# A fused layernorm, dilated attention and channel MLP: nine more constant matmuls, another order of loads, and a new hand-written order table

## The chip, the cores and the metric

The kernel runs on one core of a Trainium2 chip. That core has five engines which run side by side: PE (TensorE, matrix products into PSUM), DVE (VectorE), ACT (ScalarE), POOL (GpSimd) and SP (SyncE), which here issues the transfers between the chip's main memory and its on-chip memory. Each engine takes its instructions strictly in the order in which the program lists them, and waits on semaphores for what other engines or transfers must deliver. The metric is the device time of one execution in microseconds (us); the median of several runs is given.

## The reference

`S` is 2048 tokens of `D` = 512 channels, `H` = 32 heads of 16, a window of 8 keys two positions apart, and an MLP of width `F` = 1376.

```python
x  = A_x
xn = _layernorm(x)                      # per token, over 512 channels
qkv = xn @ wqkv                         # 512 x 1536, split in q, k, v of 32 heads
idx = pos[:, None] - arange(8) * 2      # own position and seven earlier ones, two apart
logits = einsum("bhsd,bhswd->bhsw", q, k[idx]) * scale    # masked where idx < 0
o  = einsum("bhsw,bhswd->bhsd", softmax(logits), v[idx])
s  = o @ wo
y  = _layernorm(xn)
h  = _gelu(y @ w1 + b1)                 # 512 x 1376
g  = _silu(h @ w2 + b2)                 # 1376 x 512
return x + s * g
```

## The kernel before

**Tiling.** Because the keys lie two positions apart, even and odd tokens never meet. The tokens are split in two classes `c`, each of 8 tiles of 128 tokens. The heads are split in four blocks `hb` of 8 heads (128 channels). One pair (`c`, `hb`) is a unit; there are eight, 0 to 7. A unit's projection is made by `qkv` (line 883): per tile twelve matmuls (line 909) that give q, k and v together in a PSUM bank, then an eviction to the buffer `U` by ACT (line 927) or DVE (line 923). Its attention is made by `attention` (line 960) on DVE, with POOL for some sums and ACT for the exponential. The MLP runs in four chunks of 512 tokens and 11 slices of `F`: `mlp1` (lines 1188, 1201, 1204, 1206) gives one slice of gelu(h), `mlp2` (line 1231) adds its product with `w2`. `wo_first` and `wo_last` apply `wo`, multiply by the gate and add x.

**Precision.** Each operand of a large product is kept as two float16 halves, high and low, and three products are summed. High halves are made by ACT, DVE or POOL (`split`, lines 571, 573; line 635 for `wqkv`), low ones by DVE or POOL (lines 577, 642). Before a weight is split, the sum of its squares sets a power of two as its scale: ACT squares it (line 605 for `wqkv`), PE adds the squares over the partitions (line 521) and DVE makes the scale of it.

**The head.** Two tiles of class 0, tiles 6 and 7, are loaded already transposed (`t`, line 1303). Their mean over the channels is found by DVE and one PE product for tile 6 (lines 707, 716) and by four PE products for tile 7 (line 704); DVE subtracts it (line 719), and `direct` multiplies them in float32 with block 0 of `wqkv` as loaded (line 727, four steps each). The other six tiles (`x`, line 1278) are normalised (statistics on DVE, line 675; factors on POOL, line 760; scaling on lines 786, 790 or 793). Tiles 0 to 3 are transposed by PE (line 811) and split by ACT and DVE (lines 815, 818); tiles 4 to 7 are transposed by a transfer (line 803).

**Constant matmuls.** Line 1350 multiplies two constant tiles into the bank `z0`, 256 columns, `WAKE` times. No one reads the result. Line 1465 lets ACT compute one element with exp, gelu or silu, `NTAB` times each; where the function isn't the one last used, ACT loads another table ahead of it.

**Order.** Every operation is first added to a list, `Plan.ops`, and gets its place in it as its number. `Plan.issue` (line 291) then emits the operations in the order of the table `ORDER` (line 80), which is complete: 1290 numbers. It alone decides in which order each engine and SP's queue see their work, and which buffer of a ring an operation gets. Constants such as `EV0`, `EV1` and `W1ENG` say which engine does an operation; the tuple `LOADS` only sets the numbers of the loads.

Loads have the numbers 0 to 18, the zero fills of line 1285 are 108 and 109, the constant matmuls 110 to 128. So the head of the old table, `110, 6, 4, 37, 111, 38, ...`, is a constant matmul, the load of tile 7, the load of x tile 0, the statistics of tile 0, and so on. SP issues in it: tile 7, x0, tile 6, first half of block 0 of `wqkv`, x2, x1, second half of block 0, x5, b1, block 1, x4, x3, block 1's second half, then W1's last part, x7, x6 and the rest of W1.

Of the kernel before, what the change touches and what calls it, by code (L numbers as in the profile page):

```python
# [56 lines left out]
W1ENG = ('dve', 'act', 'act', 'act', 'act', 'act', 'act')  # L57
# [4 lines left out]
EV0 = ('act', 'act', 'dve', 'act', 'dve', 'dve', 'dve', 'dve')  # L62
EV1 = ('dve', 'dve', 'act', 'dve', 'act', 'act', 'act', 'act')
# [12 lines left out]
NTAB = (8, 12, 6)  # L76
# [299 lines left out]
PU1 = 0.969  # L376
PWARM = 0.9
PEV = 0.2698

PTOT = 0.5899  # L380

WAKE = 19
PS1 = 1.1561

QHI = 4

PQLO = 0.5225

# [1187 lines left out]
```

## Time and profile before

| what | value |
|---|---|
| median of 3 runs | 409.51 us (409.25 to 409.98) |
| profiled execution | 409.47 us |
| its span, first to last instruction | 407.7 us |
| time around the span | 1.8 us |
| granted TensorE clock, mean | 0.999 |

The profile is of one execution. Its views used below are the page with the busy time of each engine, the chain of work that ended last, the timeline (start, duration, engine, line, operation, output and inputs, count; in brackets the idle time before and what ended it), busy times by stretches, and groups of instructions by line. An instruction's duration in the timeline is from its start to its end; matmuls overlap, so their pace is read from start to start. `U` in a transfer from `in_A_xt` is a transposed tile, `prod` from `in_A_x` an x tile, `prod` from `in_A_wqkv` block 0.

### The profile page before, as it was taken

How to read it: one execution, taken by the hardware profiler on the slowest of the kernel's cores; microseconds unless marked ns; L12 is line 12 of the kernel's file. 1: busy time of each engine (PE TensorE's matmuls, PEld its weight loads, DVE VectorE, ACT ScalarE, POOL GpSimd, SP SyncE). 2: the span in 40 equal slices, each digit the busy share in tenths (PEclk: the TensorE clock that was granted, in tenths of full speed). 3: DMA queues.
4: the chain of work that ended last, by engine and by line, in shares of the span. 5: the costliest groups of instructions: out<-in, count | busy, mean ns of one | idle time of the engine just before them, and what ended most of it. 6: DMA issues, size and time to landing. Idle time of an engine off the chain costs nothing.

```text
span 407.7 us, 5541 instructions
## 1 busy us (share of the span) xinstructions
PE 400.9 (98%) x2030; PEld 198.3 (49%) x2030; DVE 378.7 (93%) x386; ACT 246.2 (60%) x413; POOL 134.1 (33%) x141
## 2 busy tenths in 40 slices
PE   7999999999999999999999999999999999999996
PEld 5665544444444455445544554444455444444443
DVE  5987999999999999999799999999799899999976
ACT  3999998895599866753595344224422195367160
POOL 4823001062752443044404425052507206250012
PEclk9999999999999999999999999999999999999999
DMA  7977481440026271944092008233312466008655
GB/s 270 411 164 224 157 226 40 126 149 17 2 49 154 48 157 52 195 78 57 2 185 86 0 2 213 82 130 103 92 37 79 91 168 162 0 1 141 202 153 208
DMA packets 52627, 48.04 MB, mean 118 GB/s; under 512 B 37066, under 2 KB 37510, under 8 KB 52088
## 3 DMA queue, kind: packets, MB, share of 16 engines
q1 hardware_dynamic: 52600, 47.69, 43.2%
q8 instruction: 16, 0.26, 0.3%
q14 instruction: 11, 0.09, 0.1%
HBM read 24.40 MB, written 7.34 MB: 78 GB/s over the span
## 4 chain that ended last, share of the span: by engine, by line
PE 97%; DMA 1%; DVE 1%; SPq 0%; issue 0%; DVEq 0%
PE ps L909 30%; PE ps L1188 26%; PE z L1231 25%; PE ps L1101 5%; PE z L1133 2%; PE ps L1133 2%; PE z L1219 2%; PE pl L909 1%; DMA U<-in_A_xt_dram 1%; PE z L727 1%; PE pl L1133 1%; PE pl L727 1%; PE z L1222 1%; PE z L811 1%; DVE U L1165 0%; DVE U L1172 0%
## 5 line engine op out<-in xcount | busy, mean ns | idle before, releaser
L909 PE MATMUL ps<-wq,yT 128*128 128x384 f16 (+1 forms) x708 | 129.6, 337 | 0.0
L1231 PE MATMUL z<-w,h 128*128 128x512 f16 x480 | 113.5, 379 | 0.0
L1188 PE MATMUL ps<-yT,w 128*128 128x512 f16 x480 | 109.2, 379 | 0.0
L909 PEld LDWEIGHTS <-yT 128*128 128x128 f16 x744 | 72.6, 98 | 58.6 <-issue 0.2
L975 DVE TENSOR_TENSOR prod<-U 128x2048 f32<-128x2048 f32 x32 | 73.1, 2285 | 1.4 <-DMA U<-U 0.5
L1188 PEld LDWEIGHTS <-w 128*128 128x128 f16 x480 | 46.6, 98 | 55.9 <-issue 0.9
L978 DVE TENSOR_REDUCE L<-prod 128x128 f32<-128x2048 f32 x32 | 73.0, 2282 | 0.6
L1231 PEld LDWEIGHTS <-h 128*128 128x128 f16 x480 | 46.6, 98 | 53.9 <-issue 0.2
L927 ACT ACTIVATE U<-ps,cs 128x384 f32<-128x384 f32 x56 | 31.3, 573 | 56.8 <-PE ps L909 56.8
L1044 POOL TENSOR_TENSOR prod<-prod,prod 128x1024 f32<-128x1024 f32 x14 | 38.5, 2770 | 79.7 <-DVE prod L1033 64.0
L1033 DVE TENSOR_TENSOR prod<-pl,U 128x2048 f32<-128x2048 f32 x28 | 63.5, 2283 | 0.3
L1201 ACT ACTIVATE ps<-ps,b1T,hsc 128x512 f32<-128x512 f32 x40 | 29.7, 747 | 27.8 <-PE ps L1188 27.5
L1204 ACT ACTIVATE h<-ps,hsc 128x512 f16<-128x512 f32 x40 | 27.1, 682 | 16.7 <-PE z L1231 15.0
L1054 POOL COPY gate<-prod 1x1 f32<-1x1 f32 x21 | 4.9, 231 | 97.4 <-DVE prod L975 90.4
L1055 POOL TENSOR_TENSOR prod<-prod 128x1024 f32<-128x1024 f32 x14 | 32.9, 2348 | 0.0
L1206 DVE SCALAR_TENSOR_TENSOR h<-ps,hsc,h 128x512 f16<-128x512 f32 x40 | 29.7, 743 | 2.1 <-ACT h L1204 2.0
L1101 PE MATMUL ps<-wo,oT 128*128 128x512 f16 x96 | 21.9, 379 | 0.0
L1028 DVE TENSOR_TENSOR prod<-prod,prod 128x2048 f32<-128x2048 f32 x9 | 20.6, 2283 | 0.1
L1201 ACT ACT_TABLE_LOAD x13 | 16.7, 1283 | 3.8 <-PE ps L1188 3.7
L1465 ACT ACT_TABLE_LOAD x14 | 18.0, 1283 | 0.2
L1016 ACT ACTIVATE o<-prod,osc 128x1024 f16<-128x1024 f32 (+1 forms) x9 | 9.5, 1050 | 14.0 <-DVE prod L1028 8.3
L1055 POOL TENSOR_TENSOR prod<-prod,prod 128x1024 f32<-128x1024 f32 x7 | 16.4, 2350 | 0.0
(201 smaller groups left out, 404.2 us busy)
## 6 DMA issues: line engine op xcount, KB each, us to landing
f<-in_A_x_dram SPq DMA_DIRECT2D x31, 256.0 KB, 4.9
U<-U SPq DMA_DIRECT2D x16, 392.0 KB, 4.3
gd<-f SPq DMA_DIRECT2D x12, 256.0 KB, 3.7
prod<-in_A_x_dram SPq DMA_DIRECT2D x8, 256.0 KB, 5.3
oT<-in_B_w_dram SPq DMA_DIRECT2D x2, 1024.0 KB, 7.4
yT<-in_B_w_dram SPq DMA_DIRECT2D x2, 1024.0 KB, 6.9
f<-gd SPq DMA_DIRECT2D x8, 256.0 KB, 2.7
out_dram<-f SPq DMA_DIRECT2D x8, 256.0 KB, 3.1
```

What stands on the lines that cost most here:

```text
L909: nc.tensor.matmul(b.t[:, 0:wide], y[:, s, k, o:o + P], wq[hb][:, t, k], start=(n == 0), stop=(n == 11))
L927: act(384, lambda i=i, b=b: nc.scalar.activation(U3[:, i:i + 31:15, :], b.t[:, 0:384].rearrange("p (t e) -> p t e", t=3), AF.Identity, sca ...
L975: dve(2048, lambda p2=p2, g=g: nc.vector.tensor_tensor(p2(), q, slots(Ut, KH, 2 * g), op=ALU.mult), qk + [("kh", ub, 0), ("kh", ub, 1), (" ...
L978: dve(2048, lambda pr=pr, g=g: nc.vector.tensor_reduce(L3()[:, 2 * g:2 * g + 2], pr.t.rearrange("p (r f d) -> p r f d", r=2, d=DH), AX.X, ...
L1033: dve(2048, lambda: nc.vector.tensor_tensor(pr.t.rearrange("p (r f d) -> p r f d", r=2, d=DH), A3()[:, 2 * g:2 * g + 2].rearrange("p r (f ...
L1044: pool(2.4, lambda n=n: nc.gpsimd.tensor_tensor(acc.t[:, n:n + 1024], acc.t[:, n:n + 1024], p1.t[:, n:n + 1024], op=ALU.add), [acc, p1], [ ...
L1055: nc.gpsimd.tensor_tensor(x.t[:, 0:1024], x.t[:, 0:1024], y(), op=ALU.add)
L1101: nc.tensor.matmul(b.t, oT[:, hb, i // 4, s, i % 4], wo[:, t, hb], start=(hb == 0 and n == 0), stop=(hb == last and n == 2))
L1188: nc.tensor.matmul(b.t[0:M], w1[:, s, f * 512 + k * M:f * 512 + (k + 1) * M], yT[ch][:, t, k], start=(n == 0), stop=(n == 11))
L1201: act(512, lambda: nc.scalar.activation(b.t[0:M], b.t[0:M], AF.Gelu_apprx_tanh, bias=b1T[0:M, f:f + 1], scale=hsc[0:M, 1:2]), [b, ("b1T",) ...
L1206: dve(512, lambda: nc.vector.scalar_tensor_tensor(lo()[0:M], b.t[0:M], hsc[0:M, 2:3], hi()[0:M], op0=ALU.mult, op1=ALU.subtract), [b, hk], ...
L1231: nc.tensor.matmul(z.t, hl[s][:, t * P:(t + 1) * P], w2[:, w, f], start=(f == 0 and n == 0), stop=False)
```

## The change

Only constants change. `WAKE` goes from 19 to 28. `NTAB` goes from (8, 12, 6) to (8, 13, 7). `EV0` and `EV1` give the evictions of units 0 and 1 to other engines: for unit 0 tile 1 goes from ACT to DVE, tiles 5 and 7 from DVE to ACT; for unit 1 tiles 0 and 1 go from DVE to ACT. `W1ENG` gives the first high part of W1 (512 columns) from DVE to ACT, the second (512) and the last (384) from ACT to DVE. `ORDER` is a new table of 1301 numbers; since nine constant matmuls are added, an operation numbered 129 or more before has a number higher by nine, and after the added activations by ten or eleven.

```diff
-W1ENG = ('dve', 'act', 'act', 'act', 'act', 'act', 'act')
+W1ENG = ('act', 'dve', 'act', 'act', 'act', 'act', 'dve')
...
-EV0 = ('act', 'act', 'dve', 'act', 'dve', 'dve', 'dve', 'dve')
-EV1 = ('dve', 'dve', 'act', 'dve', 'act', 'act', 'act', 'act')
+EV0 = ('act', 'dve', 'dve', 'act', 'dve', 'act', 'dve', 'act')
+EV1 = ('act', 'act', 'act', 'dve', 'act', 'act', 'act', 'act')
...
-NTAB = (8, 12, 6)
+NTAB = (8, 13, 7)
...
 ORDER = (
-    110, 6, 4, 37, 111, 38, 112, 40, 49, 113, 0, 1, 114, 3, 8, 32, 19, 115, 109, 116, 2, 117, 118, 119, 120,
-    121, 122, 123, 124, 125, 26, 27, 20, 128, 28, 7, 18, 5, 50, 21, 54, 53, 55, 51, 33, 52, 56, 10, 68, 22, 29,
...
+    110, 0, 108, 4, 1, 111, 112, 113, 114, 115, 2, 116, 117, 19, 244, 118, 109, 119, 120, 121, 37, 122, 123, 3,
+    124, 125, 32, 137, 130, 6, 131, 20, 134, 133, 132, 8, 21, 38, 40, 33, 5, 129, 22, 54, 34, 23, 35, 24, 36,
+    53, 26, 27, 47, 10, 41, 43, 49, 55, 25, 126, 50, 28, 56, 67, 136, 172, 51, 57, 42, 9, 29, 30, 7, 45, 11, 31,
...
-WAKE = 19
+WAKE = 28
```

Read with the numbers of the operations, the new table says this of the head. SP issues tile 6, x0, both halves of block 0, x2, tile 7, x1, block 1's first half, x4, x3, x5, block 1's second half, x6, a part of W1, x7, b1 and the rest of W1. PE does nineteen constant matmuls, the mean of tile 6 (20), four constant ones, the first direct step of tile 6 (22), the sum of the first squares of block 0 (34), a direct step (23), the second sum (35), a direct step (24), tile 7's mean (26), the last direct step of tile 6 (25), a constant matmul, tile 0's transposes (50), the four direct steps of tile 7 (28 to 31) with one constant matmul among them, the first four matmuls of tile 0, two constant ones, the sum of block 1's first squares, tile 1's transposes, a constant matmul, block 1's second sum, and tile 3's transposes. Tile 2's transposes come later. ACT squares both halves of block 0 first, scales three of its quarters, squares block 1's first half, casts tile 0, scales the fourth quarter, normalises tile 1 and squares block 1's second half.

At the end, `wo_last` takes the first part of tile 4's product before the matmuls that need the last half of `oT`; in the queue of SP the last V halo of unit 6 stands behind a transposing store to `oT`.

122 rows, old and new, of the table ORDER are left out of this document.

## The prediction

> **What bounds the kernel now.** I read the busy table first, then the chain of work that ended last.
>
> ```profile
> span 407.7 us, 5541 instructions
> PE 400.9 (98%) x2030; PEld 198.3 (49%) x2030; DVE 378.7 (93%) x386; ACT 246.2 (60%) x413; POOL 134.1 (33%) x141
> ...
> PE 97%; DMA 1%; DVE 1%; SPq 0%; issue 0%; DVEq 0%
> ```
>
> PE is both the busiest engine and the chain. A busy PE can hide gaps, since matmul ends are modelled, so the next views are the busy time by stretches, PE's long wait, and two pieces of the chain in order of time.
>
> ```profile
> 0.00:5.00 5.00, 3.81 (x23) 3.03 (x24) 1.34 (x5) 1.28 (x1) 1.03 (x9) 1.00 0.54 166
> 5.00:10.00 5.00, 3.35 (x17) 2.00 (x16) 4.15 (x10) 1.97 (x4) 3.42 (x3) 1.00 1.03 369
> 10.00:15.00 5.00, 5.00 (x26) 3.02 (x25) 4.69 (x21) 4.47 (x11) 3.67 (x5) 1.00 1.05 405
> 15.00:20.00 5.00, 4.97 (x33) 3.04 (x32) 4.79 (x15) 4.97 (x10) 4.92 (x5) 1.00 1.01 416
> 20.00:30.00 10.00, 10.00 (x64) 5.99 (x63) 8.30 (x20) 9.97 (x20) 2.95 (x3) 1.00 0.69 170
> 30.00:45.00 15.00, 15.00 (x89) 8.42 (x88) 12.86 (x25) 14.97 (x32) 3.57 (x2) 1.00 0.81 259
> 45.00:403.00 358.00, 357.98 (x1784) 172.36 (x1784) 340.72 (x294) 208.54 (x341) 114.57 (x116) 1.00 0.39 98
> ```
> ```profile
> PE ps L716 <- DVE f L707: 1.6, 1, 1.6
> ```
> ```profile
> 17.00 9.10 PE ps L909 x56
> ...
> 66.50 2.59 PE ps L1188 x12
> ```
>
> Columns after the stretch: its length, PE, PEld, DVE, ACT, POOL, clock, DMA share, GB/s. From 10 us on PE is full, and in the chain twelve 512-column matmuls take 2.59 us, 0.216 each, and a 384-column one 0.162 (9.10 by 56): full pace. Nothing after 20 us can be gained from PE, only lost. What the change can win lies in the first 17 us, and the tail. The timeline of that head:
>
> ```profile
> 1.19 3.26 PE L1350 MATMUL z<-first,fours 128*128 128x256 bf16 x16 [1.19 <-DVE first L448]
> ...
> 4.08 0.69 DVE L675 BATCH_NORM_STATS2 bn<-prod 128x6 f32<-128x512 f32 x1 [2.58 <-DMA prod<-in_A_x_dram]
> ...
> 4.28 1.06 PE L704 MATMUL ps<-U,first 128*128 128x128 f32 x8
> ...
> 5.90 1.02 DVE L707 TENSOR_REDUCE f<-U 128x128 f32<-128x512 f32 x1 [0.72 <-DMA U<-in_A_xt_dram]
> ...
> 6.85 1.35 DVE L719 TENSOR_TENSOR U<-U,ps 128x512 f32<-128x512 f32 x2
> ...
> 6.98 0.84 ACT L605 ACTIVATE wq<-prod 128x768 bf16<-128x768 f32 x1 [4.97 <-DMA prod<-in_A_wqkv_dram]
> ...
> 6.98 0.49 PE L716 MATMUL ps<-f,first 128*128 128x128 f32 x2 [1.65 <-DVE f L707]
> ...
> 7.58 0.91 PE L727 MATMUL z<-prod,U 128*128 128x384 f32 x2
> ...
> 9.41 0.81 PE L727 MATMUL z<-prod,U 128*128 128x384 f32 x2
> ...
> 10.05 0.27 PE L1350 MATMUL z<-first,fours 128*128 128x256 bf16 x1
> ...
> 12.49 0.66 PE L811 MATMUL z<-first,prod 128*128 128x128 f32 x4
> ...
> 12.98 0.81 PE L727 MATMUL z<-prod,U 128*128 128x384 f32 x2
> ...
> 16.37 0.63 PE L811 MATMUL z<-first,prod 128*128 128x128 f32 x4
> ...
> 16.83 3.41 PE L909 MATMUL ps<-wq,yT 128*128 128x384 f16 x20
> ```
>
> By start to start, two L727 take 0.64 us (9.41 to 10.05), four L811 or L704, the same shape, 0.44 to 0.49, one L909 0.162. So the useful work that PE has behind it at 16.83 is 8 L704 0.9, 2 L716 0.2, 16 L727 5.2, 16 L811 1.75, 8 L909 1.3, sums of squares 0.1: 9.4 us. **7.4 us are lost**: 1.19 before the first matmul, 3.09 of constant matmuls, 1.8 waiting for tile 6, the rest single constant matmuls and short waits. The change is worth what it does to these 7.4 us, plus what it loses later.
>
> **Loads.** Tile 6 comes first instead of third, tile 7 sixth instead of first, the head block third and fourth instead of fourth and seventh. The queue's bytes set the landing: in the old order the first block half lands at 6.98 (ACT started then) behind 1152 KB; in the new one 896 KB are ahead of its end, at 369 GB/s 0.7 us sooner, 6.27. In the same way, 256 KB per 0.71 us and 384 KB per 1.07: second half 7.3, x2 8.0, tile 7 8.75, x1 9.45; from 10 us at 405 GB/s: block 1 first half 10.4, x4 11.1, x3 11.7, x5 12.4, its second half 13.35. These are estimates from the rows above. Bytes in all are the same, and the MLP weights still end the burst.
>
> **Start of the direct matmuls.** Tile 6 now goes first and lands ahead of x0, which was there at 4.08; with its 1.02 the reduce L707 ends at 4.5 to 5.1. The nineteen constant matmuls now ahead of the mean L716 end at 4.6 (16 by 4.28, three more at 0.11, half a 512-column one). DVE does x0's statistics (0.69 and a short piece), then the subtract, half of L719's 1.35: about 6.1. The first L727 waits for the block: 6.3 instead of 7.58. But in the old order PE had already done tile 7's eight mean matmuls, in a hole; now they lie among the direct ones. Lost so far: 6.3 less 0.2 useful, 6.1.
>
> **Behind it.** The new order has PE's sums of squares of block 0 between the direct matmuls, so that PE waits for ACT:
>
> ```profile
> 7.73 0.19 ACT L605 ACTIVATION_READ_ACCUMULATOR wq<-prod 128x1 f32 x1
> ...
> 11.95 0.61 ACT L635 ACTIVATE wq<-prod,qsc 128x384 f16<-128x384 f32 x1
> ...
> 14.36 0.86 POOL L760 TENSOR_TENSOR rb<-pb,halves 128x3 f32<-128x3 f32 x1
> ...
> 15.49 0.54 DVE L793 TENSOR_SCALAR prod<-prod,mv,rb 128x512 f32<-128x512 f32 x1
> ```
>
> A square with its read takes 0.94 to 1.03 us. The first ends at 7.3, PE is there at 6.95 to 7.15 (0.2 lost); the second, landed at 7.3, ends at 8.35, PE is there at 8.0 (0.4 lost). Then PE runs on: two more direct steps, tile 7's mean at 9.1 (landed 8.75), tile 0's transposes, the four direct steps of tile 7, until 13.9. Five constant matmuls stand among them and behind at 0.11: 0.55. The four L635, 0.55 each, and the first q4 squares put the scaled block ready at 13.05, in time. Last, tile 3's transposes need x5: landed 12.4, statistics 0.9, factor L760 0.86, then two other DVE pieces and L793, 15.3 to 15.65, where PE arrives at 15.35: 0 to 0.3 lost. **Sum**: 6.1 + 0.2 + 0.4 + 0.55 + (0 to 0.3) = 7.25 to 7.55, and if the first direct step runs at a slower start after the idle stretch 0.2 more. Against 7.4 before, that is -0.15 to +0.35; I take +0.1. What the earlier start wins is given back to tile 7's mean, the squares and the constant matmuls.
>
> **The nine constant matmuls.** Three more than before stand ahead of the mean, hidden by the load and the reduce, and four in the hole behind it; in the dense part there are five where there were three, the 0.55 counted. The clock column is 1.00 in 5 to 10 us although PE had just sat idle 1.65. The Trainium skill (TensorE: Matmul & The Clock Gate, Part 1) says that the clock halves after an idle window of about 3.4 us. By that rule even a hole from 4.6 to 6.3 keeps the clock without any matmul, so the additions could only cost, and rival (d) below would have no chance; the one hole of this trace agrees, but stays below that window, so that I leave (d) a small one.
>
> **Engines moved.** Of the evictions three more go to ACT net, one W1 half comes in and two leave for DVE.
>
> ```profile
> L923 DVE TENSOR_SCALAR U<-ps,cs x3: 606/609/617, 29.4 to 35.7; 128x384 f32<-128x384 f32 x3
> ...
> L573 ACT ACTIVATE w<-oT,hsc x4: 704/1132/1132, 32.9 to 37.1; 128x1024 f16<-128x1024 f32 x3, 128x512 f16<-128x512 f32 x1
> ...
> L927 ACT ACTIVATE U<-ps,cs 128x384 f32<-128x384 f32 x56 | 31.3, 573 | 56.8 <-PE ps L909 56.8
> ```
>
> ACT: three at 0.57, less one W1 half of about 0.5 (the 512 one cancels): +1.2 us, in a stage, 15 to 45, in which it is idle 0.09 us of 30. DVE loses about as much. In the order table the PE pieces behind these are also moved later (tile 4's of unit 0 by 2 us of matmuls, tiles 4 and 5 of unit 1 by 5 to 8, though tiles 6 and 7 come 3 sooner), so most of the cover is there: I take 0.2, between 0 and 1.2.
>
> **Table loads.** Counting the changes of exp, gelu and silu down the old ACT order gives 38, as many as the trace has besides the first (14 and 13 in these rows, 11 in smaller groups); the new order gives 45, the two added activations included.
>
> ```profile
> L1465 ACT ACT_TABLE_LOAD x14 | 18.0, 1283 | 0.2
> L1201 ACT ACT_TABLE_LOAD x13 | 16.7, 1283 | 3.8 <-PE ps L1188 3.7
> ```
>
> Seven times 1.283 are 9 us of ACT, nearly all after 45 us, where it is idle 149 us. They are hidden there: each is one gelu or exp that comes 1.3 us later, and PE's MLP pieces stand behind other matmuls. I take nothing; uncovered, each costs PE at most 1.3. The Trainium skill (ScalarE: Activation LUTs, What ACT_TABLE_LOAD costs) adds a drain of 1.38 us to each switch: by that page, an estimate, the seven are 19 us of ACT instead of 9, and one uncovered costs PE 2.7. No row here shows the drain; the sum would hold by either.
>
> **The tail.** Three rows of the last 16 us:
>
> ```profile
> 392.55 1.24 SPq L1021 DMA_TRANSPOSE oT<-o  x1
> ...
> 395.20 7.30 PE L1133 MATMUL z<-wo,oT 128*128 128x256 f16 x39
> ...
> 404.51 0.42 DVE L1172 TENSOR_TENSOR U<-U 128x256 f32<-128x256 f32 x1
> ```
>
> The last pieces stay as they are: twelve 256-column matmuls, L1165, L1172 at 404.51, a store that fills the rest of the span. The last half of oT is issued at 392.55 and used within the 39 matmuls from 395.20; the new order puts nine 512-column ones of tile 4 ahead of that use, 1.9 us more cover. I take nothing.
>
> **Sum.** 0.1 + 0.2 = 0.3 over the profiled execution's 409.47 (span 407.7 and 1.8 around it): 409.8; that execution is the median of the three runs within 0.04.
>
> **Rivals.** (a) *The head is shorter.* If the loads land 0.5 to 1 us ahead of my byte count, the squares stop waiting (0.6), x5's wait goes, and the first direct step starts at 6.1: 7.4 becomes 6.6, 408.7. For it: 0 to 5 us moved only 166 GB/s, and the block's rows are longer than the tiles'. Against: tile 7 then comes too late for its slot and takes back half. Chance 0.17. (b) *ACT becomes the bound of 15 to 45 us* and PE waits for evictions: slower. ACT's 1.2 us more appear whole as idle PE: 409.5 + 0.1 + 1.2 = 410.8, and with the W1 halves as late as the evictions 412.0. It decides where a piece of PE has less than 1.2 us between the eviction of its bank and its own start. For it: ACT's 14.97 of 15. Against: with ACT just as full, the old order had no PE wait there (15.00 of 15), and the pieces named above start later. Chance 0.25. (c) *A load late in the new queue order holds DVE* at unit 6, whose last V halo now stands behind oT's transpose, so that PE waits at the tail: if DVE waits for one whole landing, 4.3 us (the DMA row below), less 1.9 of new cover, PE loses 2.4: 412.2. Chance 0.06.
>
> ```profile
> U<-U SPq DMA_DIRECT2D x16, 392.0 KB, 4.3
> ```
>
> (d) *The clock falls* in the 1.1 us hole, as it stood at the start, where 16 constant matmuls took 3.09 us instead of 1.75: 1.35 lost, 411.1. The 1.65 us hole of before did not do it: chance 0.02.
>
> **Numbers.** 0.2% is 0.8 us, about what a measurement of this kernel can tell from no change. The forecast, with its own range 408.9 to 410.3, has 0.50 and is no change; (a) faster 0.17; (b), (c), (d) slower 0.33. Range 408.6 to 411.5: it holds the forecast, (a) and most of (b).
>
> **What would show it.** Right: the first L727 near 6.3; the L521 of block 0 ahead of a wait of 0.2 to 0.4 on ACT; PE 15.00 of 15 in 30 to 45, and 358 of 358 after. Wrong: a row of PE waiting for ACT L927 or DVE L1206 over 0.5 us, a first L727 after 7, or an L909 chain that starts dense before 15.5 with the same work behind it.

## The result and the profile after

| | median | lowest to highest | runs |
|---|---|---|---|
| before | 409.98 us | 409.25 to 412.19 | 9 |
| after | 414.05 us | 412.34 to 414.62 | 9 |

The ratio is 1.0083, with a 95% interval of 1.0065 to 1.0100: **slower by 0.8%**, where 409.8 (408.6 to 411.5) was predicted. The profiled execution took 414.19 us, its span is 412.4, 4.7 more than before.

The runs of both kernels fall into two groups by the granted clock, and without that the numbers below can't be read. After: four runs at a mean clock of 0.998 or more took 412.34 to 413.12, five at 0.994 to 0.996 took 414.05 to 414.62. Before, over the 120 runs that stand beside the experiments: 92 at 0.998 or more have a median of 409.75 (409.13 to 410.94), 28 at 0.990 to 0.996 have 411.75. "At full clock" means the first group from here on. At full clock the change costs 412.50 - 409.75 = 2.75 us; the rest is that more than half of its runs lose clock, against a quarter before.

The page of the new kernel, its waits of PE, and its busy times by stretches (columns as in the prediction):

```profile
span 412.4 us, 5564 instructions
PE 403.8 (98%) x2039; PEld 199.8 (48%) x2039; DVE 380.5 (92%) x384; ACT 256.2 (62%) x424; POOL 127.5 (31%) x141
```
```profile
PE ps L1189 <- DVE h L1207: 2.1, 1, 2.1
PE pl L728 <- DMA prod<-in_A_wqkv_dram: 1.2, 1, 1.2
```
```profile
5.00:10.00 5.00, 3.67 (x19) 2.09 (x18) 2.69 (x11) 1.93 (x5) 2.65 (x2) 1.00 0.95 333
...
20.00:30.00 10.00, 9.88 (x64) 5.99 (x63) 9.51 (x29) 9.69 (x18) 3.42 (x3) 1.00 0.36 99
30.00:45.00 15.00, 15.00 (x91) 8.63 (x89) 12.50 (x20) 14.90 (x30) 3.81 (x2) 1.00 0.91 243
45.00:250.00 205.00, 205.00 (x1038) 100.08 (x1036) 197.46 (x176) 151.94 (x255) 62.06 (x69) 1.00 0.37 93
250.00:300.00 50.00, 47.93 (x221) 21.82 (x219) 45.07 (x34) 18.91 (x34) 19.99 (x17) 0.97 0.29 89
300.00:400.00 100.00, 100.00 (x492) 47.20 (x491) 95.17 (x77) 48.14 (x68) 22.26 (x28) 1.00 0.41 109
```

PE is full everywhere but in the head, in 20 to 30, and in 250 to 300, where 2.07 us are missing and the clock column reads 0.97. The prediction had taken 45 to 403 us as one stretch. The timeline of that place, the new kernel first and then the old one:

```profile
245.31 1.45 SPq L942 DMA_DIRECT2D U<-U  x2
...
245.84 4.48 DVE L1034 TENSOR_TENSOR prod<-pl,U 128x2048 f32<-128x2048 f32 x2
...
250.47 6.72 POOL L1045 TENSOR_TENSOR prod<-prod,prod 128x1024 f32<-128x1024 f32 x2 [10.86 <-DVE prod L1034]
...
251.11 3.86 DVE L976 TENSOR_TENSOR prod<-U 128x2048 f32<-128x2048 f32 x1 [0.78 <-DMA U<-U]
...
255.00 2.29 DVE L979 TENSOR_REDUCE L<-prod 128x128 f32<-128x2048 f32 x1
...
257.32 2.29 DVE L1034 TENSOR_TENSOR prod<-pl,U 128x2048 f32<-128x2048 f32 x1
...
259.53 0.74 DVE L1207 SCALAR_TENSOR_TENSOR h<-ps,hsc,h 128x512 f16<-128x512 f32 x1
...
260.32 4.44 PE L1189 MATMUL ps<-yT,w 128*128 128x512 f16 x12 [2.07 <-DVE h L1207]
```
```profile
243.13 1.48 SPq L941 DMA_DIRECT2D U<-U  x2
...
244.30 4.49 DVE L1033 TENSOR_TENSOR prod<-pl,U 128x2048 f32<-128x2048 f32 x2
...
248.71 2.28 DVE L975 TENSOR_TENSOR prod<-U 128x2048 f32<-128x2048 f32 x1
248.93 6.59 POOL L1044 TENSOR_TENSOR prod<-prod,prod 128x1024 f32<-128x1024 f32 x2 [9.30 <-DVE prod L1033]
...
253.23 0.74 DVE L1206 SCALAR_TENSOR_TENSOR h<-ps,hsc,h 128x512 f16<-128x512 f32 x1
...
253.89 2.28 DVE L1033 TENSOR_TENSOR prod<-pl,U 128x2048 f32<-128x2048 f32 x1
```

Read it from the end. PE's L1189 needs a PSUM bank that DVE's L1207 frees, and L1207 starts 13.7 us behind the pair of L1034 at 245.84, where its twin of before started 8.9 behind the pair at 244.30. Three things make nearly all of the 4.8 (4.65). SP issues the two K halo copies of unit 5 at 245.31 instead of 243.13 (2.2 us later, where DVE is 1.5 later); a halo copy moves the keys of earlier tokens that a window needs from the neighbouring partition. So L976, which reads them, waits 0.78 us; before it started the moment DVE was free. That L976 takes 3.86 us instead of 2.28. And one L1034, 2.29, stands ahead of L1207 that stood behind it before.

What follows the stall, in stretches cut where the granted clock changes:

```profile
257.17:260.58 3.41, 1.34 (x8) 0.52 (x6) 3.38 (x4) 0.00 (x0) 0.01 (x1) 1.00 0.17 41
260.58:264.00 3.42, 3.42 (x10) 1.19 (x9) 3.42 (x4) 0.00 (x0) 0.00 (x0) 0.50 0.00 0
264.00:267.41 3.41, 3.41 (x18) 1.52 (x17) 2.59 (x2) 1.44 (x2) 0.00 (x0) 1.00 0.47 154
```

For 3.42 us the clock is 0.50, and eight L1189 run at 0.427 instead of 0.216 us: 1.7 us more. The account of the 4.7 us: stall 2.07, half clock 1.7, head 0.9 (at 16.63 us PE has 8.35 us of useful work behind it by the prediction's count, so 8.28 are lost against 7.4), and 0.28, from start to start of the matmuls, for a bank that an eviction frees late at 22.55; two small waits of before (0.12 and 0.19) are gone. Sum 4.6.

### The profile page after: what moved, and what is told of

It reads as the page before. It is cut to its first block, busy times and chain, and to the rows that moved or that the text cites. A ratio compares the mean times of both kernels' runs of the same rounds, so it can differ in the third digit from the quotient of the medians.

```text
span 412.4 us, 5564 instructions
## 1 busy us (share of the span) xinstructions
PE 403.8 (98%) x2039; PEld 199.8 (48%) x2039; DVE 380.5 (92%) x384; ACT 256.2 (62%) x424; POOL 127.5 (31%) x141
## 4 chain that ended last, share of the span: by engine, by line
PE 89%; DVE 5%; DMA 3%; SPq 1%; issue 1%; ACT 0%; DVEq 0%
PE ps L910 28%; PE ps L1189 24%; PE z L1232 24%; PE ps L1102 4%; PE z L1134 2%; PE ps L1134 2%; PE z L1220 2%; DMA prod<-in_A_x_dram 2%; PE pl L910 1%; DVE prod L1034 1%; DMA f<-in_A_x_dram 1%; DVE bn L676 1%; PE pl L1134 1%; PE z L1223 1%; DMA gd<-f 1%
## 5 line engine op out<-in xcount | busy, mean ns | idle before, releaser
L1189 PE MATMUL ps<-yT,w 128*128 128x512 f16 x480 | 110.6, 383 | 2.1 <-DVE h L1207 2.1
L976 DVE TENSOR_TENSOR prod<-U 128x2048 f32<-128x2048 f32 x32 | 74.7, 2336 | 3.0 <-DMA U<-U 1.4
L1189 PEld LDWEIGHTS <-w 128*128 128x128 f16 x480 | 46.9, 99 | 59.4 <-issue 5.5
L1034 DVE TENSOR_TENSOR prod<-pl,U 128x2048 f32<-128x2048 f32 x28 | 63.4, 2284 | 0.7 <-DMA U<-U 0.4
L1045 POOL TENSOR_TENSOR prod<-prod,prod 128x1024 f32<-128x1024 f32 x14 | 36.7, 2640 | 85.1 <-DVE prod L1034 67.0
L1205 ACT ACTIVATE h<-ps,hsc 128x512 f16<-128x512 f32 x40 | 27.0, 683 | 12.9 <-PE z L1232 11.2
L1207 DVE SCALAR_TENSOR_TENSOR h<-ps,hsc,h 128x512 f16<-128x512 f32 x40 | 29.2, 742 | 2.5 <-ACT h L1205 2.5
L1202 ACT ACT_TABLE_LOAD x15 | 19.2, 1283 | 13.8 <-PE ps L1189 13.6
L1056 POOL TENSOR_TENSOR prod<-prod,prod 128x1024 f32<-128x1024 f32 x7 | 16.4, 2347 | 0.0
```

The costliest lines, as they stand in the source:

```text
L976: dve(2048, lambda p2=p2, g=g: nc.vector.tensor_tensor(p2(), q, slots(Ut, KH, 2 * g), op=ALU.mult), qk + [("kh", ub, 0), ("kh", ub, 1), (" ...
L1034: dve(2048, lambda: nc.vector.tensor_tensor(pr.t.rearrange("p (r f d) -> p r f d", r=2, d=DH), A3()[:, 2 * g:2 * g + 2].rearrange("p r (f ...
L1045: pool(2.4, lambda n=n: nc.gpsimd.tensor_tensor(acc.t[:, n:n + 1024], acc.t[:, n:n + 1024], p1.t[:, n:n + 1024], op=ALU.add), [acc, p1], [ ...
L1056: nc.gpsimd.tensor_tensor(x.t[:, 0:1024], x.t[:, 0:1024], y(), op=ALU.add)
L1189: nc.tensor.matmul(b.t[0:M], w1[:, s, f * 512 + k * M:f * 512 + (k + 1) * M], yT[ch][:, t, k], start=(n == 0), stop=(n == 11))
L1202: act(512, lambda: nc.scalar.activation(b.t[0:M], b.t[0:M], AF.Gelu_apprx_tanh, bias=b1T[0:M, f:f + 1], scale=hsc[0:M, 1:2]), [b, ("b1T",) ...
```

## The experiments

Fifteen kernels, each timed in rounds with the kernel before on the same chip. Order tables of another line length shift the code: a line may stand up to three away from its number after (L1034 is L1032 in a_swap). The last columns are runs at a clock of 0.996 or less, and the median of the others.

| kernel | ratio to before, 95% | low clock | at full clock |
|---|---|---|---|
| before | | 28 of 120 | 409.75 |
| after | 1.0083 [1.0065, 1.0100] | 5 of 9 | 412.50 |
| a_swap | 1.0063 [1.0046, 1.0081] | 0 of 6 | 412.27 |
| a_halo | 1.0017 [0.9999, 1.0034] | 2 of 12 | 410.38 |
| a_pool | 1.0075 [1.0052, 1.0098] | 3 of 6 | 413.27 |
| a_pool2 | 1.0023 [1.0005, 1.0041] | 0 of 10 | 411.19 |
| b_halo | 1.0036 [1.0016, 1.0057] | 3 of 12 | 411.40 |
| a_fill | 1.0047 [1.0033, 1.0061] | 0 of 12 | 412.27 |
| b_fill | 1.0013 [1.0000, 1.0027] | 0 of 12 | 410.69 |
| h_ahead | 1.0029 [1.0014, 1.0043] | 1 of 12 | 410.98 |
| h_bhead | 0.9993 [0.9977, 1.0010] | 0 of 12 | 409.98 |
| a_const | 0.9995 [0.9979, 1.0010] | 0 of 12 | 410.26 |
| b_const | 0.9981 [0.9963, 1.0000] | 1 of 12 | 409.90 |
| b_const7 | 0.9991 [0.9975, 1.0007] | 0 of 12 | 409.83 |
| a_split | 1.0017 [1.0002, 1.0032] | 0 of 12 | 411.13 |
| a_cs | 1.0058 [1.0037, 1.0079] | 0 of 8 | 412.66 |
| a_aa | 1.0033 [1.0014, 1.0053] | 0 of 12 | 411.75 |

### What makes the stall

**a_swap** exchanges L1207 (operation 901) and the L1034 ahead of it (863):

```diff
-970, 863, 901, 913
+970, 901, 863, 913
```

> The changed kernel with one pair of VectorE's order exchanged: the L1207 that frees the PSUM bank PE waits for at 258 us goes ahead of the L1034 that stands in front of it. Theory 1 (the order of these two makes the stall): L979 ends at 257.3, L1207 frees the bank at 258.0 to 258.1, PE is there at 258.26, so the 2.07 us wait falls to 0 to 0.3 and the window at half clock behind it (1.68) goes too: span 408.6 to 409.0, time 410.4 to 410.8, and the runs no longer in two groups 1.8 apart. Rival (VectorE is late in sum, the order only chooses who pays): the wait moves to the next piece of PE that needs a bank or an h from VectorE, 2 us in all, and the time stays at 412.3 to 414.6.

Its waits of PE (the first matmul's wait left out):

```profile
PE ps L908 <- DVE f L1114: 1.2, 2, 0.9
PE pl L726 <- DVE U L718: 0.3, 1, 0.3
PE ps L1100 <- DVE h L1205: 0.3, 1, 0.3
```

The wait at 258 is gone and 1.5 us stand 10 to 50 us later, where DVE's L1114 and L1205 free other banks late. At full clock the median is 0.23 us lower, which lies within the scatter of the two (412.03 to 413.06, and 412.34 to 413.12), and no run of six has a low clock. The rival was right: DVE is late in sum, and the order only chose who pays.

**a_halo** issues the two K halo copies ahead of three other transfers; DVE's order is untouched:

```diff
-835, 808, 922, 905, 903, 857, 858, 850, 832, 859, 860, 907, 831, 289, 833, 1014
+832, 833, 835, 808, 922, 905, 903, 857, 858, 850, 859, 860, 907, 831, 289, 1014
```

> The changed kernel with the two K halo copies (L942) of unit 5's next scores issued ahead of three other transfers on SP, about 1.9 us sooner; VectorE's order stays as in the changed kernel. Theory 1 with a second cause (the late halo delays VectorE by 0.78 us, and its L976 takes 3.86 instead of 2.28 us because GpSimd's adds L1045 begin 0.64 us before it): L976 starts at 250.33, takes 2.28, and everything behind it on VectorE comes 2.36 us sooner, so that L1207 ends at 257.9 and PE waits 0 to 0.2 although L1034 still stands ahead: 410.4 to 410.8. Rival (order alone): only the 0.78 us are won, L976 stays at 3.8, PE still waits 1.3 us at 258: span 411.6, time 411.5 without the clock window, 413.3 with it.

The same two engines at that place:

```profile
250.24 2.28 DVE L974 TENSOR_TENSOR prod<-U 128x2048 f32<-128x2048 f32 x1
...
250.47 6.59 POOL L1043 TENSOR_TENSOR prod<-prod,prod 128x1024 f32<-128x1024 f32 x2 [10.86 <-DVE prod L1032]
```

L976 starts without a wait, ahead of the add, and takes 2.28 again; PE has no wait for DVE left. At full clock 2.1 us are won. So the late copies are the root: 0.78 us of waiting turned into 2.4 us of DVE, because the wait let POOL's add begin first.

**a_pool** was to show this last step by itself, with seven one-element copies on POOL ahead of the add:

```diff
+for _ in range(7):      # unit 4, first half only
+    nc.gpsimd.tensor_copy(gate, acc.t[0:1, 0:1])
 nc.gpsimd.tensor_tensor(acc.t[:, n:n + 1024], acc.t[:, n:n + 1024], p1.t[:, n:n + 1024], op=ALU.add)
```

> The changed kernel, its order untouched, with seven one-element copies on GpSimd (0.14 us each, about 1 us) ahead of unit 4's first L1045, so that this add begins after VectorE's L976 instead of 0.64 us ahead of it. Theory (of two such operations the one that begins first runs alone, and the other stands still until it ends): L976 takes 2.28 us instead of 3.86, the add is the one that is stretched, VectorE is 1.58 us sooner and PE's wait at 258 falls from 2.07 to 0.5 us; runs at full clock at 410.8 to 411.2, and no second group. Rival (L976 is slow for another reason, such as the halo that it reads): it stays near 3.9 us and the wait near 2.1.

It missed: the copies need only the first product, so they ran while POOL waited for the second anyway, and the add began at 252.10, still 0.6 us ahead of L976 (3.90 us). **a_pool2** reads the second product:

```diff
-    nc.gpsimd.tensor_copy(gate, acc.t[0:1, 0:1])
+    nc.gpsimd.tensor_copy(gate, p1.t[0:1, 0:1])
```

> The changed kernel, its order untouched, with the seven one-element copies on GpSimd now reading the second product, so that they begin only when VectorE's second L1034 has ended and the add L1045 begins about 1.6 us later, behind the start of L976. Theory (of two such operations the one that begins first runs alone): L976 takes 2.28 us instead of 3.9, the add is stretched instead, and PE's wait at 258 falls from 2.07 to about 0.5 us: 410.8 to 411.3 at full clock, and no run with a half-clock window from this place. Rival (L976 is slow for another reason, such as the halo that it reads): it stays near 3.9 us and the wait near 2.1.

```profile
250.38 3.68 POOL L1047 COPY gate<-prod 1x1 f32<-1x1 f32 x7 [10.84 <-DVE prod L1034]
...
251.03 2.29 DVE L976 TENSOR_TENSOR prod<-U 128x2048 f32<-128x2048 f32 x1 [0.78 <-DMA U<-U]
...
258.68 2.75 PE L1192 MATMUL ps<-yT,w 128*128 128x512 f16 x12 [0.50 <-DVE h L1210]
```

The copies are still as late (0.78), but L976 takes 2.29 and PE's wait is 0.50, as foretold. What stands still now is POOL, though not in the add: the seven copies take 3.68 us where they took 1.58 in a_pool, and the adds begin only at 254.02, when L976 is done. The 1.57 us belong to the add that was under way when L976 began. The Trainium skill (SBUF — State Buffer, Who interferes with whom) states such a rule: a VectorE operation with two SBUF inputs contends with a GpSimd operation that reads SBUF, the port pair that they share is an exclusive lock, and the order of issue decides which of the two waits. These rows agree with it.

**b_halo** does the one move alone, in the kernel before: operations 824, 797 and 911 go ahead of the copies 822 and 821.

> The kernel before with only SP's order changed at one place: three transfers that the change also moved go ahead of the two K halo copies of unit 5, so that these are issued about 2 us later, as in the changed kernel. Theory: L975 starts late and beside a running add, takes up to 3.9 instead of 2.28 us, VectorE is 2.0 to 2.5 us late; with before's order of VectorE, L1206 frees its bank at about 256, PE is there at 255.9, and the second L1206 is due at 258.5 and done at 259.2: PE loses 0.5 to 1.3 us, 410.3 to 411.1 at full clock. Rival (in before's order there is room for it): nothing is lost, 409.6 to 410.0.

At full clock it costs 411.40 - 409.75 = 1.65 us, somewhat above the expected range. In its trace L973 waits 2.14 us for the copies and PE 0.37 and 0.5 us for DVE: the late copies hurt in the old order of DVE as well.

```profile
251.41 6.72 POOL L1042 TENSOR_TENSOR prod<-prod,prod 128x1024 f32<-128x1024 f32 x2 [9.31 <-DVE prod L1031]
...
253.41 2.50 DVE L973 TENSOR_TENSOR prod<-U 128x2048 f32<-128x2048 f32 x1 [2.14 <-DMA U<-U]
```

The product takes 2.50 us and not up to 3.9: here the copies are issued 0.8 us behind the start of the pair of L1031, where after's are issued 0.5 ahead of it, so that the add is nearly done when the product begins. The sum is the same: 2.14 + 0.22 here, 0.78 + 1.58 in after, 0.57 + 1.79 in a_fill, 2.36 us of DVE each time. In these traces DVE loses the time to the end of the add that has begun, however late the copies come within it.

### What lies behind the stall

**a_fill** keeps the stall but lets PE work nearly up to its end, with nine matmuls more in the piece ahead of it:

```diff
-for n, (s, w) in enumerate(((0, 0), (0, 1), (1, 0))):
+for n, (s, w) in enumerate(((0, 0), (0, 1), (1, 0)) + ((0, 1), (1, 0), (1, 0)) * again):    # again = 3 for one piece
```

> The changed kernel, its order untouched, with nine 512-column matmuls more (0.216 us each, 1.94 us in all) in the piece of L1232 that stands ahead of the stalled L1189: they add three products of this piece again, so that one MLP block's sum is not the reference's. The bank is as late as before, but PE is busy nearly up to 260.3 us. If the half-clock window comes from the idle 2.07 us, the group of runs near 414.3 disappears and all lie in 412.2 to 413.2 with a clock of 0.998 or more (the holes of the head may still give one in ten). Rival (the clock falls for another reason, or the matmuls add to the time): about half of the runs stay 1.8 us above the others, or the lower group moves up by 1 to 2 us.

```profile
256.20 3.40 PE L1232 MATMUL z<-w,h 128*128 128x512 f16 x15
...
259.72 2.75 PE L1189 MATMUL ps<-yT,w 128*128 128x512 f16 x12
```

The L1189 takes 2.75 us for its twelve instead of 4.44, none of the 12 runs has a low clock against 5 of 9, and the full clock group stays at 412.27. The idle time itself costs the clock. Not each low run need come from here, though: the new head has a hole of its own (below).

The old kernel's head has such a hole too, 1.65 us. **b_fill** puts 14 more constant matmuls (`WAKE` 33) into it:

> The kernel before with 14 more constant matmuls (0.11 us each) in its 1.65 us hole at 5.3 us, ahead of the first mean L716. If the runs of before that lie near 411.4 to 412.2 are runs in which the clock fell for one window after that hole, they go, and all runs lie within 0.8 us of 409.3 to 409.6. Rival (they come from elsewhere): about one run in three stays 2 us above the others. The fastest runs stay where they are in both, within 0.3: the constants end as the mean's input comes.

No run of 12 has a low clock (28 of 120 before), so the low runs of before belong to that hole, as far as 12 runs can say. But the median moves up by 0.9 us, which was not expected. In its one trace, L715 waits until 7.52, and a load of MLP weights that lands late holds ACT for 1.48 us at 47 and PE for 0.5 us at 50; whether the constants cause either is open.

The two executions that caught the clock's fall in a head, a_pool (new head) and b_halo (old head), in stretches cut at the clock's changes:

```profile
4.01:7.42 3.41, 1.55 (x13) 1.05 (x11) 2.00 (x6) 0.00 (x0) 1.11 (x2) 1.00 0.97 330
7.42:10.84 3.42, 3.30 (x7) 1.75 (x8) 0.99 (x3) 1.87 (x4) 1.54 (x1) 0.50 1.03 393
260.01:263.42 3.41, 1.46 (x7) 0.68 (x7) 3.41 (x5) 0.00 (x0) 0.00 (x0) 1.00 0.01 2
263.42:266.83 3.41, 3.41 (x17) 1.56 (x16) 3.41 (x3) 1.44 (x2) 0.00 (x0) 1.00 0.00 0
```
```profile
4.82:8.24 3.42, 1.48 (x11) 1.05 (x10) 1.99 (x6) 0.64 (x1) 2.73 (x3) 1.00 0.90 304
8.24:11.65 3.41, 3.41 (x9) 2.26 (x9) 2.59 (x7) 1.14 (x4) 1.54 (x3) 0.50 1.05 403
```

A stretch of 3.41 us in which PE is busy 1.5 is followed by one at half clock. The third row, the stall of a_pool with PE busy 1.46, is followed by none: the border lies about there and isn't sharp in these records. So a_pool, a low run of the new head with its stall of 2.07 us untouched, lost its clock in the head and not at the stall. The old head's own profile, with 1.76 busy in such a stretch, kept its clock:

```profile
3.98:7.39 3.41, 1.76 (x15) 1.46 (x13) 2.52 (x5) 0.41 (x1) 1.94 (x2) 1.00 0.97 306
```

### The rest: 0.6 us at full clock

a_halo is still 0.63 us above before. **h_ahead** is the old kernel with the first 139 entries of the new table, **h_bhead** the new one (with a_halo's move) behind the first 115 entries of the old table:

> The kernel before with the head of the changed one: its loads, its 28 constant matmuls and its order up to the third 20 of L910 (about 20 us), then the order, evictions and tables of before. Theory: the head's loss of 0.86 us reaches the end whole: span 408.5 to 408.9, time 410.3 to 410.7. Rival (the later body has room and the loss is made up, or the eviction wait belongs to the head's timing): 409.3 to 409.7, or 410.9 where an eviction wait of 0.3 comes in as well.

> The old head (loads, 19 constant matmuls, order up to the first L928 at about 20 us) with the evictions, tables and the whole later order of the changed kernel, the halo copies moved as in a_halo. Theory (the 0.6 us that are left of the loss lie in the head): 409.6 to 410.0 at full clock, as before. Rival (a part lies in the later body, in the seven table loads or the evictions): 410.1 to 410.5.

h_ahead has 410.98, near the expected time with an eviction wait; but in its trace PE is busy only 9.58 of the 10 us from 20 to 30, where the two orders are joined (9.88 after), so it can't say what the head alone costs. h_bhead has 409.98, 0.40 below a_halo and 0.23 above before. So about two thirds of the 0.6 would lie in the head and the rest in the later order, but the runs scatter (409.17 to 411.62, and 409.86 to 411.01 for a_halo), so the shares are not settled. In a_halo's own trace the later order loses 0.28 us at 22.1 and 0.30 at 398.8, where PE waits for the last transposed `oT`; before had 0.31 in two waits that are gone. The wait for `oT`, 0.26 to 0.39 from start to start of the matmuls, also stands in a_const, a_split, a_swap and a_cs. In a_split:

```profile
399.14 4.38 PE L1132 MATMUL z<-wo,oT 128*128 128x256 f16 x21 [0.23 <-DMA oT<-o]
```

The trace of h_bhead is of its slowest run, 411.62, and shows where that run lost its time: a load of MLP weights lands late, ACT squares it late, and PE waits.

```profile
51.10 1.91 ACT L510 ACTIVATE w<-yT 128x2048 bf16<-128x2048 f32 x1 [1.75 <-DMA yT<-in_B_w_dram]
...
53.15 0.17 PE L524 MATMUL z<-s,fours 128*128 128x6 bf16 x1 [1.56 <-ACT w L510]
```

**a_const** (on a_halo) puts the five constant matmuls of the dense part into the hole behind the first mean; **b_const** does the same with before's three, **b_const7** with four more:

> The changed kernel with the halo copies moved as in a_halo, and with its five constant matmuls of the dense part (0.11 us each) put into the hole behind the first mean instead. Theory: in the dense part each costs its 0.11, in the hole nothing, so the head is 0.3 to 0.55 us shorter than a_halo's (a part comes back as a longer wait for tile 3's input): the runs at full clock go from about 410.25 to 409.7 to 409.95, level with the kernel before; and with a hole of 0.2 to 0.7 us instead of 1.2, no run with the clock below 0.997. Rival (the waits behind take all of it back): 410.1 to 410.4 as a_halo.

> The kernel before with the three constant matmuls of its dense part put into its 1.65 us hole at 5.3 us. Theory: 0.33 us less than before, 409.2 to 409.7 at full clock, and as the hole is still 1.3 us, about one run in four or somewhat fewer lies 1.7 us higher at a clock of 0.996 or less. Rival (constants in front of the mean delay it, or what follows waits longer): 409.9 to 410.5, as the 14 constants of b_fill did.

> The kernel before with seven constant matmuls in its hole at 5.3 us: the three of the dense part as in b_const and four more. Theory: 0.77 us of the hole are filled and 0.5 to 1 us is left, too short for the clock to fall; nothing is delayed: 409.2 to 410.2 in all runs, none with a clock below 0.997, 0.2 to 0.4% below before's median over all its runs. Rival (the 14 of b_fill delayed something that is not the hole): 410.3 to 411.

The rival was right in a_const: the constant matmuls in the dense part cost nothing that can be seen, 410.26 against 410.38, and 409.90 and 409.83 against 409.75. In a_const's trace PE waits 0.31 us for tile 3's input and 0.20 for a square instead. In the hole they keep the clock: b_fill and b_const7, with 14 and 7 of them there, have no low run in 24, against 28 in 120. None of 12 in a_const against 2 of 12 in a_halo, and one of 12 in b_const, decide nothing. Neither b_const (0.9981) nor b_const7 (0.9991) is surely faster than before; no version beats both kernels beyond doubt.

**a_split** loads the second half of the head block behind x2 (operation 2 behind operation 3):

> a_halo with the second half of the head block loaded behind x2 instead of directly behind the first half. Theory of the prediction (the bytes ahead set a landing): the first half lands as before, ScalarE's first square at 6.1 to 6.8, and the second half comes 0.7 us later, so that PE waits 0.5 us more for its square: 410.7 to 411.1 at full clock. Rival (transfers in flight share the engines, and a transfer right behind slows the one in front): the first half lands about 0.5 us sooner, at 5.5 to 6.2, and the time is 410.0 to 410.5.

```profile
5.65 0.84 ACT L604 ACTIVATE wq<-prod 128x768 bf16<-128x768 f32 x1 [3.64 <-DMA prod<-in_A_wqkv_dram]
...
7.78 0.84 ACT L604 ACTIVATE wq<-prod 128x768 bf16<-128x768 f32 x1 [1.20 <-DMA prod<-in_A_wqkv_dram]
```

The first half landed early, the second late, and the median is that of the prediction's theory, 0.75 above a_halo. But the trace is of a run of 410.43, one of three in twelve below 410.5, and PE waits 0.50 us for a square in it as in a_halo's, so it doesn't show where the other nine lose their time. Nor can it be concluded from one execution that the first half was sped up: landings scatter by 1.5 us (below).

**a_cs** and **a_aa** (on a_halo) try to bring the first eviction forward, whose bank PE waits for at 22.55. a_cs moves POOL's L774 and DVE's L891 (operation 138, the eviction's scales) ahead of two statistics, a_aa the chain of L770 (operation 89) ahead of two additions:

> a_halo with L891 (the scales of the first evictions) moved on VectorE ahead of the two statistics L676 of tiles 6 and 7 that the new order puts in front of it. Theory: the first L928 starts at 20.4 instead of 21.9, PE's wait of 0.28 us at 22.55 goes and reaches the end: 409.8 to 410.1 at full clock against a_halo's 410.25. Rival (the evictions are late because ScalarE is full, as the prediction's rival (b) had it): the wait stays 0.2 to 0.3 us, there or at the next eviction, and the time at 410.2 to 410.4.

> a_halo with the chain of the tile factors (L770, 1 us on VectorE) moved ahead of the two additions L818 that stand in front of it, so that it starts at 17.8 instead of 19.0 and GpSimd's L774 behind it at 19.0 instead of 20.2. Theory (this chain makes the eviction late): the first L928 starts at 21.7, when ScalarE is done with its L636, instead of 21.9, and PE's wait at 22.55 falls from 0.28 to 0.1: 410.2 to 410.3 at full clock. Rival (the additions moved back by 1 us are needed sooner): PE waits for yT at 19.9 instead, up to 0.9 us, 410.4 to 411.3.

```profile
21.38 0.23 DVE L889 TENSOR_SCALAR cs<-cT,qsc 128x6 f32<-128x6 f32 x1 [1.47 <-POOL cT L772]
```
```profile
PE ps L908 <- DVE yT L817: 0.6, 1, 0.6
PE pl L908 <- DVE U L922: 0.5, 1, 0.5
```

Both lose. In a_cs (first row) DVE now stands 1.47 us idle for POOL, work that the two statistics had covered, and PE waits 1.4 and 0.5 us for evictions that DVE makes later; 2.3 us are lost. In a_aa the wait at 22.55 is gone, and PE waits 0.56 for an addition at 19.2 and 0.5 for an eviction at 36; since PE now comes 0.6 us later to that bank, this proves little. In after's trace ACT stands idle just ahead of that eviction, for DVE's scales:

```profile
21.92 0.58 ACT L928 ACTIVATE U<-ps,cs 128x384 f32<-128x384 f32 x1 [0.24 <-DVE aa L770]
```

So 0.24 of the 0.28 us come by way of DVE and POOL, not because ACT is full; but no cheaper order was found, and the 0.28 us stay.

## Why the prediction was wrong, step by step

- **PE is the bound, and only lost time counts**: right. Outside the head, 22.55 and 258 us, PE is as full as before.
- **The loads**: the first half of the head block was to land 0.7 us sooner, 6.27 for 6.98. Over ten executions of the new head ACT's first square starts at 5.90 to 7.43, median 6.57; over six of the old at 6.98 to 7.60, median 7.42. The difference by bytes was about right, 0.85. But the one profile of before was the earliest of six, so that its level was taken too low by 0.4 (the new one came out 0.3 too low), and a scatter as large as the gain was not in the sum.
- **The head's sum of +0.1, engines moved +0.2**: 0.3 in all, against about 0.4 for the head (h_bhead against a_halo, within their scatter), and 0.63 with all that is left. In the profiled execution the head lost 0.85 more than before: the block landed late in that run, and the first direct step came at 6.95 where 6.3 was forecast. The term of the constant matmuls, 0.55, was mis-sized: moving them away wins nothing that can be seen, since what PE waits for behind them comes no sooner. The eviction wait is 0.28 where 0.2 was taken; that is luck, since the scales of the eviction were late and not ACT.
- **Table loads and the tail**: the trace has 46 table loads where before had 39, ACT is busy 10 us more, and no wait of PE for ACT appears behind 45 us: right. At the end PE waits for nothing in after's trace; but in five other traces of the new order it waits 0.26 to 0.39 us for the last `oT`, so the term taken as nothing was only nearly that.
- **The step that failed** is the one that let the sum end at 45 us. For the later order the prediction went through the evictions of units 0 and 1, the table loads, the tail, and one halo, unit 6's V copy. It did not put the new order of SP beside the old one at every halo. At unit 5 two K halo copies had moved behind three other transfers, 2.2 us later and 0.6 later against DVE. Rival (c) had the mechanism, a copy late in the queue that holds DVE, but at another unit, with DVE's lateness equal to the copy's, and a chance of 0.06; that its 412.2 lies near the 412.50 at full clock is luck. Here 0.78 us of lateness became 2.4 on DVE (a_pool2) and 2.07 on PE.
- **The clock**: rival (d) had a fall in a hole for 1.35 us and a chance of 0.02, since the 1.65 us hole of before kept its clock. One execution did not show that: in a quarter of its runs it does not keep it. By the Trainium skill (TensorE: Matmul & The Clock Gate, Part 1) an idle window of about 3.4 us is needed; here a window in which PE was still busy 1.34 to 1.55 of 3.41 us was enough, three times of four, and the measurement decides. Five of nine runs of the new kernel lost clock. The one of them with a trace lost it at the stall, 1.7 us; with the stall filled none of 12 did (a_fill), with the stall removed 2 of 12 (a_halo), so most of the five belong to the stall, and one or two may belong to the head.

## What to carry to other kernels

When a whole order changes, compare the order of the transfer queue against the consumers at every unit, not only where the change is said to be: a copy that comes 0.8 us late cost VectorE three times that, because GpSimd's add began meanwhile. Don't cure such a stall by exchanging the operations that stand in its way; find what made the engine late, since moved lateness comes back at the next bank. And price a hole on PE by the clock as well: one of 1.5 to 2 us can cost as much again, in some runs and not in others, which a single profile doesn't tell.

## What the runs showed of the hardware

- The granted clock changes in steps of 3.41 us. It falls to 0.50 for one step after one in which PE was busy 1.34, 1.48 and 1.55 us; it stayed at 1.00 after 1.46 and 1.76.
- Where the steps lie differs from run to run, and with it the start. In a_halo the four constant matmuls at 5.62 us take 1.06 us and still run at half pace; after's, at 5.12, take 0.60:

```profile
5.62 1.06 PE L1349 MATMUL z<-first,fours 128*128 128x256 bf16 x4
```
```profile
5.12 0.60 PE L1351 MATMUL z<-first,fours 128*128 128x256 bf16 x4
```

- VectorE's two-input product of 2048 columns and GpSimd's two adds of 1024 don't share: begun ahead of the adds the product took 2.28 us and they 6.59 (before), begun inside the first add it took 3.86 (after). Where the adds began last of all, at 254.02 in a_pool2, they took 4.65.
- The first half of the head block in the same head is ready for ACT within a range of 1.5 us from execution to execution (5.90 to 7.43, ten traces), a range nearly twice as wide as what its reordering wins (0.85).
